# Feed-forward on one core: low parts of weights to VectorE, maximum to ScalarE, Silu as one function, smaller pieces between products

## The chip, the cores and the metric

The kernel runs on one core of one Trainium2 chip. The metric is the device time of one execution in microseconds. The kernel before was timed three times: 859.63, 856.85 and 858.03 us, a median of 858.03 us.

## What is computed

Clustered attention over 2 batches, 8 heads, 768 positions of width 64, and then two feed-forward layers on the 1536 x 512 result. The part that the change touches:

```
# first feed-forward: 512 -> 2048 -> 512
h = x @ w_in
g = np.maximum(h, 0.0) + np.log1p(np.exp(-np.abs(h)))
x = g @ w_out
# second: 512 -> 1536 -> 512
g = x @ w_gate
silu = g * (1.0 / (1.0 + np.exp(-g)))
out = (silu * (x @ w_val)) @ w_out
```

The four weights arrive in float64, the rest in float32.

## The kernel before, in words

Every float32 operand of a product is split into a high part, which TensorE takes in its rounded float32 form (`F32R`), and a low part, what is left; a product is three products (high x high, high x low, low x high), all into one PSUM bank.

A weight of 128 x 512 numbers is loaded as pairs of 32-bit words, narrowed to float32 by integer work and split. `w_narrow` takes the absolute value of the upper words on ScalarE (L122), clamps and shifts on VectorE (L123, L126) and joins the words on VectorE (L130, L133). `w_split` casts the high part `whi` on VectorE (L142) and subtracts for the low part `wlo` on GpSimd (L143). There are two buffers for the narrowed weight `m`, three for the loaded words and three or four for each split weight.

The first feed-forward works in 16 units (`h_unit`, 128 hidden columns each) and 8 groups (`y_group`, two units each). A unit is 36 matmuls of 128 x 512 (L738) into three PSUM banks; ScalarE writes |h| from each bank (L795) and VectorE max(h, 0) (L796); then exp and log on ScalarE (L799, L800), the sum on VectorE (L803), and the split of the sum: a cast on ScalarE (`gh`, L776) and a subtraction on GpSimd (`gl`, L777). A y group has four pieces of 18 matmuls (L820) into three banks each; VectorE adds every bank to an accumulator (L834); the first group is copied by ScalarE (L832), and the last group also splits the finished accumulator (`YH`, `YL`; L836, L838). PSUM's eight banks go round: a bank is used again eight allocations later. So in the middle of the stage TensorE does two units (72 matmuls) and then four pieces (72 matmuls), 144 matmuls in all; below this is called a group of the stage. Units 0 and 1 come first, units 2g+2 and 2g+3 before y group g.

The second feed-forward is built alike: 12 units (`a_unit`) of a gate and a value product, sigmoid on ScalarE (L882), two multiplies on VectorE (L883, L894), a split (L900 on ScalarE, L901 on GpSimd), and 6 groups of output products (L920) with accumulation on VectorE (L932).

The order on each engine is the order in which the program is written: every engine takes its instructions one after the other. Weight work and the softplus tails are small tasks in one queue (`todo`), which `pump` takes from after each half of a unit and after each piece: two tasks if more than four are waiting, else one. A weight is two tasks, `first` (L122, L123, L126) and `second` (L130, L133, L142, L143, and the next weight's load on the SyncE queue). A unit adds two: `log_part` (L799, L800) and `sum_part` (L803, L776, L777). With the two weights of a unit they are queued as log, first and second of an output weight, sum, first and second of an input weight. `need` takes tasks out of turn until a weight or a split sum that a product asks for is there; `first_do` puts the last two units' tails ahead of all but a weight that has begun.

Of the kernel before, what the change touches and what calls it, by code (L numbers as in the profile page):

```python
# [15 lines left out]
AF = mybir.ActivationFunctionType  # L16
ALU = mybir.AluOpType
# [12 lines left out]
def _r(t):  # L30

    return t.bitcast(F32)
# [8 lines left out]
def kernel(  # L41
# [18 lines left out]
    nc = tc.nc  # L60
# [48 lines left out]
    def w_narrow(loaded):  # L109

        raw, shape, wide = loaded
        if not wide:
            yield
            yield raw
            return
        lo, hi = raw[:, :, :, 0], raw[:, :, :, 1]  # L120
        m = wp.tile(shape, I32, tag="m", name="m", bufs=2)
        nc.scalar.activation(out=m.bitcast(F32), in_=hi.bitcast(F32), func=AF.Abs)  # L122
        nc.vector.tensor_scalar(  # L123
            out=m.bitcast(F32), in0=m.bitcast(F32), scalar1=F64_LEAST, scalar2=F64_MOST, op0=ALU.max, op1=ALU.min
        )
        nc.vector.tensor_scalar(  # L126
            out=m, in0=m, scalar1=3, scalar2=0x3FFFFFF8, op0=ALU.logical_shift_left, op1=ALU.bitwise_and
        )
        yield
        nc.vector.scalar_tensor_tensor(  # L130
            out=m, in0=hi, scalar=-0x40000000, in1=m, op0=ALU.bitwise_and, op1=ALU.bitwise_or
        )
        nc.vector.scalar_tensor_tensor(  # L133
            out=m, in0=lo, scalar=29, in1=m, op0=ALU.logical_shift_right, op1=ALU.bitwise_or
        )
        yield m.bitcast(F32)

    def w_split(x, pool, tag, bufs):
        shape = list(x.shape)
        hi = pool.tile(shape, F32R, tag="h" + tag, name="whi", bufs=bufs)  # L140
        lo = pool.tile(shape, F32R, tag="l" + tag, name="wlo", bufs=bufs)
        nc.vector.tensor_copy(hi, x)  # L142
        nc.gpsimd.tensor_tensor(out=lo, in0=x, in1=_r(hi), op=ALU.subtract)  # L143
        return hi, lo

    def cols_of(w, f):
# [9 lines left out]
    def first_of(u):  # L156
        if u < NF1:
            return [(("in", u), cols_of(w_in, u), "a")]
        if u < NU:
            return [(("gate", u - NF1), cols_of(w_gate, u - NF1), "a"), (("val", u - NF1), cols_of(w_val, u - NF1), "c")]  # L160
        return []
# [15 lines left out]
    batches = [first_of(u) for u in range(3)] + [batch_of(u) for u in range(NU)]  # L177
# [9 lines left out]
            loaded_t[stream[n_load[0]][0]] = w_load(*stream[n_load[0]][1])  # L187
            n_load[0] += 1

    begun = set()  # L190

    def split_tasks(batch):

        steps = {}

        def first(key):
            while key not in loaded_t:
                load_ahead(len(loaded_t) + 1)
            steps[key] = w_narrow(loaded_t.pop(key))
            next(steps[key])  # L200

        def second(key, tag):
            x = next(steps[key])
            load_ahead(3)
            pool, bufs = pool_of[tag]
            W[key] = w_split(x, pool, tag, bufs)

        tasks = []
        for key, _, tag in batch:
            tasks.append(functools.partial(first, key))  # L210
            tasks.append(functools.partial(second, key, tag))
            begun.add(tasks[-1])
        return tasks


    todo = collections.deque()

    def first_do(tasks):

        begun_one = [todo.popleft()] if todo and todo[0] in begun else []  # L220
        todo.extendleft(reversed(begun_one + tasks))

    def pump(n=None):
        for _ in range(n or (2 if len(todo) > 4 else 1)):
            if todo:
                todo.popleft()()

    def need(table, key):
        while key not in table:
            todo.popleft()()  # L230
        return table[key]
# [393 lines left out]
    for half in range(2):  # L625
# [5 lines left out]
        for hh in range(2):  # L631
            g = 2 * C * hh
            if half == 0:
                nc.vector.tensor_scalar(
                    out=QT[hh][64:64 + C, 0, cols], in0=_r(ps)[g:g + C, 0:384], scalar1=FAR, scalar2=-FAR,
# [3 lines left out]
            else:  # L639
                nc.scalar.copy(KT[hh][64:64 + C, 0, cols], _r(ps)[64 + g:64 + g + C, 0:384])  # L640
                nc.scalar.activation(
                    out=QT[hh][64:64 + C, 0, cols], in_=_r(ps)[g:g + C, 0:384], func=AF.Identity,
# [89 lines left out]
    def proj(xh, xl, w, banks, kks):  # L732

        hi, lo = w
        for kk in kks:
            for wt, xt, last in ((hi, xh, 0), (hi, xl, 0), (lo, xh, 1)):
                for c in range(NCH):
# [5 lines left out]
                        stop=(kk == KD - 1 and last == 1),  # L743
                    )


    h0 = [bank() for _ in range(NCH)]
    w0 = need(W, ("in", 0))
# [24 lines left out]
    def split_g(g, tag):  # L773
        gh = gp.tile([128, NTOK], F32R, tag="gh", name=tag + "h")
        gl = gp.tile([128, NTOK], F32R, tag="gl", name=tag + "l")
        nc.scalar.copy(gh, g)  # L776
        nc.gpsimd.tensor_tensor(out=gl, in0=g, in1=_r(gh), op=ALU.subtract)  # L777
        return gh, gl
# [5 lines left out]
    def h_unit(f, banks=None):  # L784
        if banks is None:
            banks = [bank() for _ in range(NCH)]
            w = need(W, ("in", f))
            for half in range(2):
                proj(XH, XL, w, banks, range(2 * half, 2 * half + 2))
                pump()  # L790
        e = tp.tile([128, NTOK], F32, tag="e", name="e")
        r = tp.tile([128, NTOK], F32, tag="s", name="r")
        for c in range(NCH):
            cs = slice(512 * c, 512 * c + 512)
            nc.scalar.activation(out=e[:, cs], in_=banks[c], func=AF.Abs)  # L795
            nc.vector.tensor_scalar_max(r[:, cs], banks[c], 0.0)  # L796

        def log_part():
            nc.scalar.activation(out=e, in_=e, func=AF.Exp, scale=-1.0)  # L799
            nc.scalar.activation(out=e, in_=e, func=AF.Ln, bias=1.0)  # L800

        def sum_part():
            nc.vector.tensor_tensor(out=e, in0=r, in1=e, op=ALU.add)  # L803
            g_t[f] = split_g(e, "g")

        return [log_part, sum_part], split_tasks(batches.pop(0))

    def y_group(g):
        last = g == NF1 // 2 - 1
# [30 lines left out]

    soft0, split0 = h_unit(0, h0)
    soft1, split1 = h_unit(1, h1)
    todo.extend(split0 + [soft0[0], soft1[0], soft0[1], soft1[1]] + split1)
    pump(6)
    for g in range(NF1 // 2):
        if 2 * g + 2 < NF1:
            for f in (2 * g + 2, 2 * g + 3):
                soft, split = h_unit(f)
                if f < NF1 - 2:
                    todo.extend([soft[0]] + split[:2] + [soft[1]] + split[2:])  # L850
                else:
                    first_do(soft + split[:2])
                    todo.extend(split[2:])
        else:
            YH = keep.tile([128, KD, NTOK], F32R, tag="xh", name="YH")
            YL = keep.tile([128, KD, NTOK], F32R, tag="xl", name="YL")
        y_group(g)
# [6 lines left out]
    def a_unit(f):  # L864
        gb = [bank() for _ in range(NCH)]
        wg = need(W, ("gate", f))
        vb = None
        if f == 0:
            vb = [bank() for _ in range(NCH)]
            wv = need(W, ("val", f))  # L870
            proj(YH, YL, wg, gb, range(KD - 1))
            proj(YH, YL, wv, vb, range(KD - 1))
            proj(YH, YL, wg, gb, range(KD - 1, KD))
            proj(YH, YL, wv, vb, range(KD - 1, KD))
        else:
            for half in range(2):
                proj(YH, YL, wg, gb, range(2 * half, 2 * half + 2))
                pump()
        sg = tp.tile([128, NTOK], F32, tag="e", name="sg")
        for c in range(NCH):  # L880
            cs = slice(512 * c, 512 * c + 512)
            nc.scalar.activation(out=sg[:, cs], in_=gb[c], func=AF.Sigmoid)  # L882
            nc.vector.tensor_tensor(out=sg[:, cs], in0=gb[c], in1=sg[:, cs], op=ALU.mult)  # L883
        if vb is None:
            vb = [bank() for _ in range(NCH)]
            wv = need(W, ("val", f))
            for half in range(2):
                proj(YH, YL, wv, vb, range(2 * half, 2 * half + 2))
                pump()
        ah = gp.tile([128, NTOK], F32R, tag="gh", name="ah")  # L890
        al = gp.tile([128, NTOK], F32R, tag="gl", name="al")
        for c in range(NCH):
            cs = slice(512 * c, 512 * c + 512)
            nc.vector.tensor_tensor(out=sg[:, cs], in0=vb[c], in1=sg[:, cs], op=ALU.mult)  # L894
            if f == NF2 - 1:
                nc.scalar.copy(ah[:, cs], sg[:, cs])
                nc.vector.tensor_tensor(out=al[:, cs], in0=sg[:, cs], in1=_r(ah)[:, cs], op=ALU.subtract)

        def split_part():
            nc.scalar.copy(ah, sg)  # L900
            nc.gpsimd.tensor_tensor(out=al, in0=sg, in1=_r(ah), op=ALU.subtract)  # L901
            a_t[f] = (ah, al)

        if f < NF2 - 1:
            todo.append(split_part)
        else:
            a_t[f] = (ah, al)
        if batches:
            todo.extend(split_tasks(batches.pop(0)))
# [67 lines left out]
```

## Time and profile before

| | |
|---|---|
| median of three runs | 858.03 us |
| profiled execution | 860.54 us |
| its span (first to last instruction) | 858.4 us |
| mean granted TensorE clock | 0.984 |
| TensorE matmul busy (PE) | 815.9 us, 95% |
| VectorE (DVE) | 686.3 us, 80% |
| ScalarE (ACT) | 397.7 us, 46% |
| GpSimd (POOL) | 336.1 us, 39% |

The span has three stages: attention to about 264 us, the first feed-forward to about 559, the second to about 855. Times in rows are microseconds from the start of the span, durations microseconds or, where marked mean, nanoseconds. A number in square brackets behind a row of the timeline is the idle time of that engine just before, with what ended it.

### The profile page before, as it was taken

What the parts mean: (1) busy time and instruction counts of PE and PEld (TensorE: products, weight loads), DVE (VectorE), ACT (ScalarE), POOL (GpSimd) and SP (SyncE); (2) the same over time, 40 slices, a digit from 0 to 9 for tenths busy, and PEclk for the clock granted to TensorE, in tenths of its full rate; (3) what the DMA queues carried; (4) which work ended last, traced back from release to release, by engine and by line L of the source; (5) the groups of instructions that cost most, each with busy time, mean ns of one, the idle gap of its engine ahead of it and who ended that gap; (6) DMA issues with size and microseconds to landing.
All of it is one profiled execution on the core that took longest, in us unless ns stands there. A gap on an engine that the chain in (4) does not pass through costs nothing.

```text
span 858.4 us, 11743 instructions
## 1 busy us (share of the span) xinstructions
PE 815.9 (95%) x4366; PEld 700.4 (82%) x4366; DVE 686.3 (80%) x1016; ACT 397.7 (46%) x735; POOL 336.1 (39%) x229
## 2 busy tenths in 40 slices
PE   7899999999999899989898997899999999999998
PEld 6899999999888678768677786678888888888886
DVE  6889988898886778898888887848886868876464
ACT  4589888988883755434244434133312213120210
POOL 4636565545421645444244333324433222332110
PEclk9899999999999999999999998999999999999999
DMA  8966776575212132122121120102222221211003
GB/s 201 263 144 148 184 169 145 131 178 119 71 38 69 52 95 74 56 76 82 59 73 50 49 74 25 49 25 74 74 74 74 74 74 50 74 56 43 1 1 147
DMA packets 65336, 75.42 MB, mean 88 GB/s; under 512 B 28960, under 2 KB 51584, under 8 KB 65280
## 3 DMA queue, kind: packets, MB, share of 16 engines
q1 hardware_dynamic: 65280, 74.68, 31.7%
q8 instruction: 34, 0.56, 0.3%
q14 instruction: 22, 0.18, 0.1%
HBM read 48.27 MB, written 3.19 MB: 60 GB/s over the span
## 4 chain that ended last, share of the span: by engine, by line
PE 66%; DVE 24%; issue 4%; ACT 3%; DMA 2%; POOL 1%; SPq 0%; DVEq 0%; POOLq 0%; ACTq 0%
PE bank L738 29%; PE bank L920 11%; PE ops L522 7%; PE tps L505 6%; PE sps L473 6%; DVE m L123 5%; DVE acc L834 4%; PE bank L820 3%; DVE e L803 3%; DVE m L133 2%; DVE r L796 2%; DVE m L130 2%; PE sims L384 2%; DVE whi L142 1%; DVE m L126 1%
## 5 line engine op out<-in xcount | busy, mean ns | idle before, releaser
L143 POOL TENSOR_TENSOR wlo<-m,whi 128x512 fp32r<-128x512 f32 x68 | 100.6, 1480 | 290.2 <-DVE whi L142 275.4
L123 DVE TENSOR_SCALAR m<-m 128x512 f32<-128x512 f32 x68 | 87.0, 1279 | 38.0 <-ACT m L122 38.0
L512 DVE TENSOR_TENSOR tl<-tps,th 128x384 fp32r<-128x384 f32 x192 | 98.9, 551 | 16.4 <-ACT th L511 16.0
L481 DVE TENSOR_REDUCE nm<-sps 128x1 f32<-128x768 f32 x96 | 91.4, 953 | 14.2 <-PE sps L473 11.3
L505 PE MATMUL tps<-id,p 128*128 128x128 f32 x576 | 94.5, 281 | 1.0 <-DVE tl L512 1.0
L511 ACT CAST th<-tps 128x384 fp32r<-128x384 f32 x192 | 84.7, 492 | 20.1 <-PE tps L505 17.3
L489 ACT ACTIVATE p<-sps,nm 128x768 f32<-128x768 f32 x96 | 88.3, 920 | 5.2 <-DVE nm L481 5.1
L473 PE MATMUL sps<-KT,QT 128*128 128x384 f32 x384 | 84.1, 341 | 5.8 <-ACT p L489 5.0
L738 PE MATMUL bank<-YH,whi 128*128 128x512 f32 x288 | 81.7, 392 | 2.6 <-DVE acc L834 2.6
L505 PEld LDWEIGHTS tps<-id,p 128*128 128x128 f32 x576 | 76.3, 153 | 7.8 <-DVE tl L512 4.3
L738 PE MATMUL bank<-YL,whi 128*128 128x512 f32 x288 | 81.4, 391 | 0.0
L738 PE MATMUL bank<-YH,wlo 128*128 128x512 f32 x288 | 81.3, 391 | 0.0
L522 PE MATMUL ops<-th,VV 128*128 128x256 f32 x288 | 80.6, 308 | 0.0
L776 ACT CAST gh<-e 128x1536 fp32r<-128x1536 f32 x16 | 23.7, 1481 | 121.8 <-DVE e L803 121.8
L820 PE MATMUL bank<-gh,whi 128*128 128x512 f32 x192 | 58.2, 404 | 17.7 <-DVE r L796 8.6
L522 PE MATMUL ops<-tl,VV 128*128 128x256 f32 x288 | 73.2, 283 | 0.0
L122 ACT ACTIVATE m<-raw 128x512 f32<-128x512 f32 x68 | 44.3, 663 | 61.2 <-POOL wlo L143 61.2
L777 POOL TENSOR_TENSOR gl<-e,gh 128x1536 fp32r<-128x1536 f32 x16 | 57.2, 3579 | 36.2 <-ACT gh L776 32.4
L473 PEld LDWEIGHTS sps<-KT,QT 128*128 128x128 f32 x384 | 63.8, 191 | 6.6 <-ACT p L489 5.6
L738 PEld LDWEIGHTS bank<-YH,whi 128*128 128x128 f32 x288 | 54.5, 189 | 14.3 <-issue 3.0
L738 PEld LDWEIGHTS bank<-YL,whi 128*128 128x128 f32 x288 | 54.5, 189 | 11.4
L738 PEld LDWEIGHTS bank<-YH,wlo 128*128 128x128 f32 x288 | 54.4, 189 | 11.3
(124 smaller groups left out, 1778.6 us busy)
## 6 DMA issues: line engine op xcount, KB each, us to landing
raw<-in_moe_w_out_dram SPq DMA_DIRECT2D x28, 512.0 KB, 3.3
raw<-in_moe_w_in_dram SPq DMA_DIRECT2D x16, 512.0 KB, 3.8
QT<-hi SPq DMA_DIRECT2D x32, 192.0 KB, 3.0
raw<-in_moe_w_val_dram SPq DMA_DIRECT2D x12, 512.0 KB, 4.7
raw<-in_moe_w_gate_dram SPq DMA_DIRECT2D x12, 512.0 KB, 3.4
KT<-hi SPq DMA_DIRECT2D x14, 384.0 KB, 4.2
qn<-in_q_dram SPq DMA_DIRECT2D x16, 192.0 KB, 4.9
kn<-in_k_dram SPq DMA_DIRECT2D x16, 192.0 KB, 3.7
```

Of the source, the lines that this page charges most:

```text
L123: nc.vector.tensor_scalar(out=m.bitcast(F32), in0=m.bitcast(F32), scalar1=F64_LEAST, scalar2=F64_MOST, op0=ALU.max, op1=ALU.min)
L143: nc.gpsimd.tensor_tensor(out=lo, in0=x, in1=_r(hi), op=ALU.subtract)
L473: nc.tensor.matmul(ps[:, c, 0:384], lhsT=Q[:, a, 128 * j:128 * j + 128], rhs=K[:, a, 384 * c:384 * c + 384], start=(a == 0), stop=(a == 1),)
L481: nc.vector.tensor_reduce(out=nm, in_=ps[:, :, 0:384], axis=AX.XY, op=ALU.max, negate=True)
L489: nc.scalar.activation(out=_h(p), in_=s_t.pop(i)[:, :, 0:384], func=AF.Exp, bias=nm_t.pop(i), accum_out=sm_t[pr][:, j:j + 1],)
L505: nc.tensor.transpose(ps[:, 128 * j:128 * j + 128], p[:, 128 * kb:128 * kb + 128], id32)
L511: nc.scalar.copy(th, pv)
L512: nc.vector.tensor_tensor(out=tl, in0=pv, in1=_r(th), op=ALU.subtract)
L522: nc.tensor.matmul(o[:, 0:CW], lhsT=VV_t[pr][:, hh, kb].rearrange("p a d -> p (a d)"), rhs=t[:, kb, :], start=(kb == 0 and lohi == 0), sto ...
L738: nc.tensor.matmul(banks[c], lhsT=wt[:, kk, :], rhs=xt[:, kk, 512 * c:512 * c + 512], start=(kk == 0 and wt is hi and xt is xh), stop=(kk ...
L820: nc.tensor.matmul(banks[NCH * d + c], lhsT=wt[:, 0, ds_], rhs=gt[:, 512 * c:512 * c + 512], start=(ff == 0 and n == 0), stop=(ff == 1 and ...
L920: nc.tensor.matmul(bk, lhsT=lhs[:, ts_], rhs=rhs[:, 0, :], start=(ff == 0 and n == 0), stop=(ff == 1 and n == 2),)
```

## The change

Five edits: (1) from the first feed-forward on, `wlo` is subtracted on VectorE; (2) from unit 3 on, max(h, 0) is a Relu on ScalarE; (3) Silu is one function of ScalarE, in place of a sigmoid and a multiply on VectorE; (4) a weight has three tasks: L122 alone, then L123 and L126, then the rest; the softplus tail has three: log, sum, split; (5) `pump` takes up to three tasks where more than twelve are waiting; a first task of a weight is not counted, and is also taken at the end of a turn when it stands next.

```diff
         nc.scalar.activation(out=m.bitcast(F32), in_=hi.bitcast(F32), func=AF.Abs)
+        yield
         nc.vector.tensor_scalar(
...
+    low_on = [nc.gpsimd]
...
-        nc.gpsimd.tensor_tensor(out=lo, in0=x, in1=_r(hi), op=ALU.subtract)
+        low_on[0].tensor_tensor(out=lo, in0=x, in1=_r(hi), op=ALU.subtract)
...
-        def second(key, tag):
+        def second(key):
+            next(steps[key])
+
+        def third(key, tag):
             x = next(steps[key])
...
             tasks.append(functools.partial(first, key))
-            tasks.append(functools.partial(second, key, tag))
+            firsts.add(tasks[-1])
+            tasks.append(functools.partial(second, key))
+            begun.add(tasks[-1])
+            tasks.append(functools.partial(third, key, tag))
             begun.add(tasks[-1])
...
     def pump(n=None):
-        for _ in range(n or (2 if len(todo) > 4 else 1)):
+        for _ in range(n or (3 if len(todo) > 12 else 2 if len(todo) > 4 else 1)):
+            if todo and todo[0] in firsts:
+                todo.popleft()()
             if todo:
+                todo.popleft()()
+            if todo and todo[0] in firsts and n is None:
                 todo.popleft()()
...
+    low_on[0] = nc.vector
+
 
     h0 = [bank() for _ in range(NCH)]
...
-            nc.vector.tensor_scalar_max(r[:, cs], banks[c], 0.0)
+            if f < 3:
+                nc.vector.tensor_scalar_max(r[:, cs], banks[c], 0.0)
+            else:
+                nc.scalar.activation(out=r[:, cs], in_=banks[c], func=AF.Relu)
...
             nc.vector.tensor_tensor(out=e, in0=r, in1=e, op=ALU.add)
+
+        def split_part():
             g_t[f] = split_g(e, "g")
 
-        return [log_part, sum_part], split_tasks(batches.pop(0))
+        return [log_part, sum_part, split_part], split_tasks(batches.pop(0))
...
-                    todo.extend([soft[0]] + split[:2] + [soft[1]] + split[2:])
+                    todo.extend([soft[0]] + split[:3] + [soft[1]] + split[3:6] + [soft[2]] + split[6:])
                 else:
-                    first_do(soft + split[:2])
-                    todo.extend(split[2:])
+                    first_do(soft + split[:3])
+                    todo.extend(split[3:])
...
-            nc.scalar.activation(out=sg[:, cs], in_=gb[c], func=AF.Sigmoid)
-            nc.vector.tensor_tensor(out=sg[:, cs], in0=gb[c], in1=sg[:, cs], op=ALU.mult)
+            nc.scalar.activation(out=sg[:, cs], in_=gb[c], func=AF.Silu)
```

`first_do` now leaves in front all steps of a weight that has begun (up to two) instead of one, and the tails of units 0 and 1 are queued as logs, sums, splits between the weights of the two units, with eight tasks taken at once there instead of six.

## Rows read from the trace of the kernel before

**Rows 1.** Windows by stage: length, each engine's busy time (instructions), granted clock, DMA.
```profile
264.35:559.40 295.05, 268.17 (x1136) 215.59 (x1136) 251.94 (x330) 125.71 (x154) 120.86 (x56) 0.98 0.21 64
559.40:854.60 295.20, 295.20 (x1294) 243.98 (x1294) 212.37 (x304) 60.06 (x87) 83.41 (x45) 0.99 0.18 57
```

**Rows 2.** Chain that ended last, a piece in the second feed-forward: start, length, what.
```profile
626.12 16.32 PE bank L920 x72
```

**Rows 3.** Waits in the first feed-forward: total us, times, longest us.
```profile
DVE m L123 <- ACT m L122: 27.1, 15, 3.6
...
PE bank L820 <- DVE r L796: 8.6, 4, 4.0
...
PE bank L820 <- DVE acc L834: 7.5, 5, 2.6
...
PE bank L738 <- DVE acc L834: 4.9, 3, 2.2
```

**Rows 4.** Timeline of TensorE, two of its stops.
```profile
301.60 0.50 PE L820 MATMUL bank<-gh,whi 128*128 128x512 f32 x1 [1.90 <-DVE r L796]
...
385.22 0.50 PE L738 MATMUL bank<-XH,whi 128*128 128x512 f32 x1 [2.25 <-DVE acc L834]
```

**Rows 5.** Windows around stops; the clock is the third number from the end.
```profile
290.00:310.00 20.00, 18.10 (x80) 14.67 (x79) 12.39 (x18) 13.32 (x20) 12.59 (x5) 1.00 0.19 53
...
370.00:390.00 20.00, 17.36 (x68) 13.85 (x69) 19.40 (x28) 5.49 (x5) 7.46 (x3) 0.91 0.20 65
...
512.00:560.00 48.00, 38.03 (x152) 29.51 (x151) 38.75 (x49) 13.93 (x18) 18.54 (x11) 0.93 0.16 51
```

**Rows 6.** Timeline around one sum, TensorE left out: start, length, instruction.
```profile
375.03 1.75 DVE L803 TENSOR_TENSOR e<-r,e 128x1536 f32<-128x1536 f32 x1
...
376.81 1.49 ACT L776 CAST gh<-e 128x1536 fp32r<-128x1536 f32 x1 [9.80 <-DVE e L803]
...
378.38 3.52 POOL L777 TENSOR_TENSOR gl<-e,gh 128x1536 fp32r<-128x1536 f32 x1 [0.43 <-ACT gh L776]
...
378.90 3.28 DVE L123 TENSOR_SCALAR m<-m 128x512 f32<-128x512 f32 x1 [0.33 <-ACT m L122]
...
382.22 0.43 DVE L126 TENSOR_SCALAR m<-m 128x512 int32<-128x512 int32 x1
...
382.68 0.69 DVE L130 SCALAR_TENSOR_TENSOR m<-raw,m 128x512 int32<-128x512 int32 x1
...
384.13 0.43 DVE L142 CAST whi<-m 128x512 fp32r<-128x512 f32 x1
...
384.48 1.88 DVE L834 TENSOR_TENSOR acc<-bank,acc 128x512 f32<-128x512 f32 x3
...
386.27 0.42 DVE L123 TENSOR_SCALAR m<-m 128x512 f32<-128x512 f32 x1
```

**Rows 7.** Groups by line in the first feed-forward: count, busy us, mean ns, idle before.
```profile
L123 DVE TENSOR_SCALAR m<-m 128x512 f32<-128x512 f32 x36 | 53.6, 1489 | 27.1 <-ACT m L122 27.1
...
L796 DVE TENSOR_SCALAR r<-bank 128x512 f32<-128x512 f32 x48 | 30.0, 681 | 6.1 <-ACT e L795 6.1
...
L126 DVE TENSOR_SCALAR m<-m 128x512 int32<-128x512 int32 x36 | 26.1, 724 | 1.2
...
L795 ACT ACTIVATE e<-bank 128x512 f32<-128x512 f32 x48 | 25.0, 594 | 13.9 <-PE bank L738 12.0 <-POOL gl L777 1.9
```

**Rows 8.** Groups by line in the second feed-forward.
```profile
L883 DVE TENSOR_TENSOR sg<-bank,sg 128x512 f32<-128x512 f32 x36 | 22.6, 681 | 22.0 <-ACT sg L882 22.0
...
L897 DVE TENSOR_TENSOR al<-sg,ah 128x512 fp32r<-128x512 f32 x3 | 2.1, 693 | 2.1 <-ACT ah L896 2.1
...
L882 ACT ACT_TABLE_LOAD x1 | 1.3, 1283 | 0.0
```

**Rows 9.** Timeline: the same subtraction on GpSimd and on VectorE at one time.
```profile
565.16 1.30 POOL L838 TENSOR_TENSOR YL<-acc,YH 128x512 fp32r<-128x512 f32 x1 [0.17 <-ACT YH L836]
...
565.72 1.28 DVE L838 TENSOR_TENSOR YL<-acc,YH 128x512 fp32r<-128x512 f32 x1 [0.69 <-ACT YH L836]
```

More of the change, by code (lines that the diff above doesn't have):

```diff
@@ L122, in w_narrow @@
         nc.scalar.activation(out=m.bitcast(F32), in_=hi.bitcast(F32), func=AF.Abs)
+        yield
         nc.vector.tensor_scalar(
@@ L188, in load_ahead @@
             n_load[0] += 1
-    begun = set()
+    firsts, begun = set(), set()
     def split_tasks(batch):
@@ L218, in first_do @@
     def first_do(tasks):
-        begun_one = [todo.popleft()] if todo and todo[0] in begun else []
-        todo.extendleft(reversed(begun_one + tasks))
+        begun_ones = []
+        while todo and todo[0] in begun:
+            begun_ones.append(todo.popleft())
+        todo.extendleft(reversed(begun_ones + tasks))
     def pump(n=None):
-        for _ in range(n or (2 if len(todo) > 4 else 1)):
+        for _ in range(n or (3 if len(todo) > 12 else 2 if len(todo) > 4 else 1)):
+            if todo and todo[0] in firsts:
+                todo.popleft()()
             if todo:
+                todo.popleft()()
+            if todo and todo[0] in firsts and n is None:
                 todo.popleft()()
@@ L842 @@
     soft1, split1 = h_unit(1, h1)
-    todo.extend(split0 + [soft0[0], soft1[0], soft0[1], soft1[1]] + split1)
-    pump(6)
+    todo.extend(split0 + [soft0[0], soft1[0], soft0[1], soft1[1], soft0[2], soft1[2]] + split1)
+    pump(8)
     for g in range(NF1 // 2):
```

## The prediction

> **What bounds the kernel now.** I read the stretches first. From 559.40 to 854.60 TensorE is busy for all of 295.20 us [rows 1], at the full-speed spacing of 16.32 us for 72 matmuls, 0.2267 us each [rows 2]: the second feed-forward hides everything else, and edits there can only cost. From 264.35 to 559.40, the first feed-forward, TensorE is busy for 268.17 of 295.05 us, so it stands idle for 26.9 us; its 1136 matmuls at full spacing are 257.5 us, so the busy time holds another 10.7 us of slow matmuls. 37.5 us is all that can be won there. Who ends the idle time: the waits say VectorE, 8.6 us for `r` (the maximum with zero), 7.5 and 4.9 us for `acc` [rows 3], that is, for PSUM banks that VectorE empties late. The slow matmuls follow long stops: after the stop of 1.90 us [rows 4] the granted clock stayed at 1.00, after 2.25 us it was 0.91 over the window, and over the 48 us with the longest stop, 4.0 us [rows 3], 0.93 [rows 5], the engine falling from 2.4 to 1.2 GHz for a while; 0.09 of 20 us is 1.8 us for such a fall.
>
> Why VectorE is late stands in the timeline [rows 6]. After the sum (375.03, 1.75 us) the next task in the queue is the beginning of another weight. Its `m` (L122) is on ScalarE behind `gh`, 1.49 us, so VectorE's L123 starts 2.1 us after the sum; by then `gl` (378.38, 3.52 us) runs on GpSimd, and L123 lasts 3.28 us, ending with it, where it takes 0.42 us alone. So one sum costs VectorE about 5 us. Over the stretch: L123 1.489 us in the mean, x36, against 0.42 alone is 38.5 us; L126, 0.724 against 0.43, 10.6 us (beside `wlo` on GpSimd) [rows 7]; waiting for `m` 27.1 us [rows 3].
>
> A check: one group (two h units and the four y pieces, 144 matmuls, 32.64 us of TensorE) asks of VectorE twelve evictions of `acc` (1.88 us for three: 7.5), two sums (3.5), six maxima (3.76), four weights of 0.42+0.43+0.69+0.69+0.43 (L133 like L130 [rows 6]) and 0.03 between them (11.2): 26.0. With an eighth of 49 us held and of 27.1 us waiting it is 35.5 us; the stretch divided by eight is 36.9. VectorE is the bound of the first feed-forward.
>
> **The change, part by part.**
> Maximum to ScalarE, units 3 to 15: takes 13 times 1.88 = 24.4 us from VectorE, 3.76 per group. ScalarE pays three ACTIVATEs from PSUM, nearest row `Abs` at 0.594 shown, about 0.53 behind each other [rows 7]: 1.6 us a unit, 20.6 in all, on an engine busy 125.7 of 295 us [rows 1]. Hidden as long as a unit's `Abs` and maximum (3.2 us) aren't stuck behind a `gh` that waits for a sum; without that cover a bank comes late by that wait. The wait for `r` goes; the bank is then freed by ScalarE, which waits for products 12.0 us in the stretch [rows 7]. The Trainium skill ("ScalarE: Activation LUTs", Rules for kernel authors) says the opposite, maximum on VectorE. By that rule the 24.4 us stay on VectorE and a group asks 3.76 us more of it than below; here rows decide, 0.594 against 0.681 from PSUM, on the engine that has time.
>
> Low parts to VectorE: 36 weights in this stretch [rows 7]. VectorE's own subtraction of this shape is 0.693 us (`al`, L897) [rows 8], 0.65 in a queue: 23.4 us, 2.6 a group. Bounds: 0.6, and 1.28 as beside a GpSimd subtraction [rows 9]; I take 0.65, because a low part follows a cast that has then already waited. It takes `wlo` off GpSimd, so L126's 10.6 us go.
>
> Pieces: the `Abs` is now issued ahead of its pump's end, and `gh`/`gl` are a task of their own after the next weight. So most of the 27.1 us go (I keep up to 2 us a group, where `Abs` sits behind log and exp, two ACTIVATEs of `gh`'s size [rows 6], 3 us). The holding does not go: ScalarE does not wait for the pump, so `gh` still starts when the sum ends, and `gl` covers 1.6 to 5.1 us after it. What now meets it is not L123 (0.1 to 0.5) but L142, the cast, at 2.4: VectorE loses about 2.9 us per sum instead of 5, between 0 (where evictions fill the time) and 3.5 (`gl`'s length). Twice a group: 5.8.
>
> VectorE per group after: 7.5 + 3.5 + four weights of 3.46 (13.8) = 24.8, held 5.8, waiting 0 to 2: 31 to 33 against TensorE's 32.64. TensorE is the bound again, barely, and bursts decide the rest.
>
> The bursts, from the order of the queue. With over 12 tasks waiting a pump takes three. After y piece 0 of groups 1, 2 and 4 these are the sum, and both other steps of an output weight. Take the end of that piece as 0: `acc` to 1.9, sum to 3.6, L123 and L126 to 4.5, L130 and L133 to 6.0, L142 held until 8.7 and done at 9.1, low part 9.8, first bank of the next `acc` 10.5. TensorE has eight banks and takes three per piece: it wants that bank at the third matmul of piece 3, at 2 x 4.08 + 0.45 = 8.6. A stop of 1.9 us. Groups 3 and 5 begin with steps of a weight and lose less, about 1.5; I take 9 us for the five.
> Start: the stop of 1.90 us at 301.60 [rows 4] waits for unit 3's `r`, which ScalarE now writes; with smaller ones before it I leave 1 us.
> End: from 512 to 560 us TensorE's 152 matmuls need 34.5 of 48 us [rows 5]: 13.5 us lost. The stop of 4.0 us waited for `r` [rows 3] and goes. In the last y group a piece asks of VectorE 1.88 for `acc`, 0.7 of waiting for `YH` (a cast like `whi`'s, on ScalarE) and 0.7 for `YL` (as L897 [rows 8]): 3.3. Four pieces are 13.2, two more weights 6.9, held some 2 beside GpSimd's part of `YL` (1.30 [rows 9]): 22 against TensorE's 16.3, 6 late, with 1 brought along 7 us.
> Slow clock: two stops over 2.25 us, 1.8 us each: 3.6.
> Left: 1 + 9 + 7 + 3.6 = 20.6 of 37.5. Gain 17.
>
> Second feed-forward: low parts add 30 x 0.65 = 19.5 us, Silu in one function removes 36 multiplies of 0.63 (22.7) [rows 8]: nothing, on an engine busy 212 of 295 us. ScalarE's Silu I price as the sigmoid; one table load of 1.28 us stands in the shadow of the first product [rows 8]; even two per unit would be 31 us on an engine busy 60 of 295 [rows 1]. Attention keeps its order (its two pumps still take one weight each).
>
> Sum: the profiled execution 860.54 (span 858.4), less 17 is 843.5; it lies 2.5 above the median of 858.03, so the forecast is 841 for the median.
>
> **The rivals.**
> (1) Bursts are absorbed: `gl` meets evictions, not the cast; stops only at start and end, 8 us and one fall of the clock, 9.8 left. Gain 27.5, 830.5. For: 31 us against 32.6; against: `gh` follows the sum by itself.
> (2) Stops of 1.9 grow just over 2.25 us, and each brings the slow clock: 2.3 + 1.8 in five groups are 20.5, 1 + 7 at the ends with 3.6 of slow clock: 32 left. Gain 5.5, 852.5. For: 1.90 and 2.25 lie close, my count of the cast is good to some 0.3 us.
> (3) Slower: three tasks per pump put the bank's release behind a burst in every middle group, each a stop as long as the longest of now, 4.0 us, and 1.8 of slow clock: six groups 34.8, start and end 8 and 3.6: 46.4 left, 9 more than now, 867. It decides once a middle group loses over (37.5 - 11.6)/6 = 4.3 us. Against: VectorE would have to ask over 36.9 us a group, and `gl` alone can hold it for no more than 7.
> (4) Nothing: ScalarE, now alone on the h banks, sits behind a waiting `gh`, so that the 20 us that TensorE waits for `r` and `acc` [rows 3] come back as waits for ScalarE: 37 left, 858.
>
> **How the numbers follow.** Forecast 0.55 (own range 833 to 848), (1) 0.18, (2) 0.15, (3) 0.07, (4) 0.05. A measurement tells 0.3%, 2.6 us. Faster 0.88, same 0.05, slower 0.07. The range leaves out the outer quarters of (1) and (2), and (3) and (4): 827 to 853.
>
> **What would show it.** Right: the second feed-forward busy throughout; L126 at 0.43 everywhere; L123's mean under 0.8; waits of TensorE for `r` gone after unit 2; casts (L142) of 2 to 3 us beside `gl`; stops under 2 us at the third matmul of a piece 3; first feed-forward 275 to 280 us. Wrong: TensorE waiting for `e` or `r` of ScalarE, a granted clock under 0.95 in many slices, the casts at 0.43 throughout, or idle TensorE after 560 us.

## The result

The changed kernel takes 845.36 us (median of four runs, 844.71 to 847.81) against 858.83 us for the kernel before on the same chip: a ratio of 0.9844 (0.9806 to 0.9883). The forecast was 841 us, the range 827 to 853. The profiled execution, the slowest of the four, took 847.81 us, its span 846.0 us. In the changed kernel's lines L756 is the projection, L845 the y piece, L123 the absolute value, L125 and L128 clamp and shift, L132 and L135 the joins, L148 the cast `whi`, L149 the low part `wlo`, L796 `gh`, L797 `gl`, L826 the sum, L859 `acc`, L817 and L819 the maximum on VectorE and on ScalarE.

Windows of the two feed-forwards, as in [rows 1]:

```profile
264.93:547.27 282.34, 266.47 (x1136) 216.44 (x1136) 245.98 (x327) 145.74 (x193) 65.94 (x20) 0.97 0.22 67
547.27:842.18 294.91, 294.90 (x1294) 243.74 (x1294) 196.87 (x298) 60.14 (x87) 42.88 (x14) 1.00 0.17 57
```

The first went from 295.05 to 282.34 us; the second still has TensorE busy throughout. Of the 24.8 us above the 257.5 us of full-speed matmuls, 15.9 are idle time. What ended most of it, to be read against [rows 3]:

```profile
PE bank L845 <- DVE acc L859: 6.6, 5, 1.8
PE bank L756 <- DVE acc L859: 4.2, 2, 3.3
PE bank L845 <- DVE r L817: 3.2, 1, 3.2
```

The other 1.9 us are two waits for the cast `whi`. One wait for `r` is left, and the stops for `acc` are six of at most 1.8 us and a last one of 3.3. The window of [rows 3] ends before the last stop of the kernel before, the one at 559.40 us; from 264 to 560 us that kernel shows

```profile
PE bank L738 <- DVE acc L834: 7.5, 4, 2.6
```

so the last stop has grown, from 2.6 to 3.3 us. VectorE's groups, against [rows 7]:

```profile
L148 DVE CAST whi<-m 128x512 fp32r<-128x512 f32 x36 | 38.7, 1074 | 1.8
L125 DVE TENSOR_SCALAR m<-m 128x512 f32<-128x512 f32 x36 | 31.0, 860 | 20.9 <-ACT m L123 20.8
L149 DVE TENSOR_TENSOR wlo<-m,whi 128x512 fp32r<-128x512 f32 x36 | 24.9, 692 | 1.9
...
L128 DVE TENSOR_SCALAR m<-m 128x512 int32<-128x512 int32 x36 | 19.5, 542 | 1.2
```

The clamp fell from a mean of 1489 to 860 ns and the shift from 724 to 542, but the cast, 0.43 us alone, now has a mean of 1074: (1.074 - 0.43) x 36 = 23.2 us. Much of the holding moved from the clamp to the cast, and little of it went: the clamp is still held for (0.860 - 0.42) x 36 = 15.8 us and the shift for 4.0, 43 us in all against 49 before. Of the 16 `gl`, seven now meet a cast (3.6 us each) and five a clamp alone (3.3 to 3.7). The chain of waits of the changed kernel around a stop shows it (start, length, what):

```profile
375.46 1.67 DVE e L826
377.13 0.35 DVE m L125
...
377.96 0.70 DVE m L132
...
378.69 0.71 DVE m L135
...
379.42 3.64 DVE whi L148
...
383.08 0.69 DVE wlo L149
383.77 0.61 DVE acc L859
...
384.43 1.65 PE bank L845 x6
```

The 6.6 us from the clamp to the end of the low part stand between a sum and the `acc` that TensorE waits for, and 3.64 of them are one cast.

### The profile page after: what moved, and what is told of

Same layout as the page of the kernel before. It is cut to its first block, busy times and chain, and to the rows that moved or that the text cites. A ratio compares the mean times of both kernels' runs of the same rounds, so it can differ in the third digit from the quotient of the medians.

```text
span 846.0 us, 11685 instructions
## 1 busy us (share of the span) xinstructions
PE 817.6 (97%) x4366; PEld 704.3 (83%) x4366; DVE 663.1 (78%) x1007; ACT 417.7 (49%) x774; POOL 240.7 (28%) x163
## 4 chain that ended last, share of the span: by engine, by line
PE 75%; DVE 16%; DMA 4%; ACT 2%; issue 2%; POOL 1%; SPq 0%; POOLq 0%; DVEq 0%; ACTq 0%
PE bank L756 34%; PE bank L944 12%; PE bank L845 8%; PE ops L540 6%; PE sps L491 6%; PE tps L523 6%; DVE acc L859 3%; DVE whi L148 2%; DVE m L125 2%; PE sims L402 2%; DMA rd<-R 2%; DVE m L135 1%; DMA R<-rd 1%; DVE e L826 1%; DVE m L132 1%
## 5 line engine op out<-in xcount | busy, mean ns | idle before, releaser
L797 POOL TENSOR_TENSOR gl<-e,gh 128x1536 fp32r<-128x1536 f32 x16 | 59.9, 3746 | 204.7 <-ACT gh L796 191.6
L925 POOL TENSOR_TENSOR al<-sg,ah 128x1536 fp32r<-128x1536 f32 x11 | 38.6, 3507 | 207.0 <-ACT ah L924 207.0
L529 ACT CAST th<-tps 128x384 fp32r<-128x384 f32 x192 | 84.7, 491 | 20.6 <-PE tps L523 18.0
L491 PE MATMUL sps<-KT,QT 128*128 128x384 f32 x384 | 86.6, 348 | 4.1 <-ACT p L507 2.3
L756 PE MATMUL bank<-YH,whi 128*128 128x512 f32 x288 | 81.4, 390 | 3.3 <-DVE acc L859 3.3
L125 DVE TENSOR_SCALAR m<-m 128x512 f32<-128x512 f32 x68 | 58.9, 866 | 31.4 <-ACT m L123 31.3
L756 PE MATMUL bank<-YL,whi 128*128 128x512 f32 x288 | 81.5, 392 | 0.0
L756 PE MATMUL bank<-YH,wlo 128*128 128x512 f32 x288 | 81.4, 391 | 0.0
L123 ACT ACTIVATE m<-raw 128x512 f32<-128x512 f32 x68 | 44.5, 667 | 72.7 <-DVE wlo L149 72.7
L918 DVE TENSOR_TENSOR sg<-bank,sg 128x512 f32<-128x512 f32 x36 | 22.8, 684 | 60.8 <-PE bank L756 60.8
L491 PEld LDWEIGHTS sps<-KT,QT 128*128 128x128 f32 x384 | 65.5, 196 | 5.4 <-ACT p L507 3.2
L845 PE MATMUL bank<-gh,whi 128*128 128x512 f32 x192 | 58.0, 407 | 11.0 <-DVE acc L859 6.6
L756 PEld LDWEIGHTS bank<-YH,whi 128*128 128x128 f32 x288 | 54.2, 188 | 15.0 <-issue 3.7
L756 PEld LDWEIGHTS bank<-YH,wlo 128*128 128x128 f32 x288 | 54.5, 189 | 11.4
L756 PEld LDWEIGHTS bank<-YL,whi 128*128 128x128 f32 x288 | 54.5, 189 | 11.3
```

The source lines that it names most:

```text
L125: nc.vector.tensor_scalar(out=m.bitcast(F32), in0=m.bitcast(F32), scalar1=F64_LEAST, scalar2=F64_MOST, op0=ALU.max, op1=ALU.min)
L491: nc.tensor.matmul(ps[:, c, 0:384], lhsT=Q[:, a, 128 * j:128 * j + 128], rhs=K[:, a, 384 * c:384 * c + 384], start=(a == 0), stop=(a == 1),)
L529: nc.scalar.copy(th, pv)
L756: nc.tensor.matmul(banks[c], lhsT=wt[:, kk, :], rhs=xt[:, kk, 512 * c:512 * c + 512], start=(kk == 0 and wt is hi and xt is xh), stop=(kk ...
L845: nc.tensor.matmul(banks[NCH * d + c], lhsT=wt[:, 0, ds_], rhs=gt[:, 512 * c:512 * c + 512], start=(ff == 0 and n == 0), stop=(ff == 1 and ...
```

## The experiments

Each ratio is to runs of the kernel before on the same chip, with its 95% interval. Rows come from different chips, whose medians of the kernel before lie between 858.48 and 859.96 us, so a difference of two rows in microseconds is good to some 1.5 us.

| kernel | us | ratio |
|---|---|---|
| changed | 845.36 | 0.9844 (0.9806 to 0.9883) |
| maximum on VectorE | 854.84 | 0.9957 (0.9942 to 0.9971) |
| low parts on GpSimd | 832.35 | 0.9697 (0.9678 to 0.9717) |
| pieces as before | 855.36 | 0.9969 (0.9955 to 0.9984) |
| sigmoid and multiply | 843.96 | 0.9840 (0.9796 to 0.9884) |
| pieces alone | 838.51 | 0.9747 (0.9706 to 0.9787) |
| gate for `gl`, one tile more | 849.74 | 0.9891 (0.9867 to 0.9914) |
| gate for `gl`, no tile more | 835.34 | 0.9717 (0.9679 to 0.9756) |
| low parts on GpSimd, split at once | 839.00 | 0.9769 (0.9752 to 0.9787) |
| low parts on GpSimd, unit 2 on ScalarE | 832.50 | 0.9698 (0.9679 to 0.9718) |
| `gl` on VectorE | 827.95 | 0.9640 (0.9621 to 0.9658) |
| `gl` on VectorE, low parts on GpSimd | 826.35 | 0.9599 (0.9563 to 0.9635) |
| `gl` on VectorE, empty last group | 821.90 | 0.9562 (0.9528 to 0.9597) |

**Each part undone.** First the maximum:

```diff
-            if f < 3:
+            if f < NF1:
                 nc.vector.tensor_scalar_max(r[:, cs], banks[c], 0.0)
```

> The changed kernel with the maximum with zero left on VectorE in all units. The theory that VectorE's demand decides: 3.76 us more per group of 32.6 us, about 35 instead of 31 us, so VectorE becomes the bound again and the middle groups lose 3 to 4 us each instead of 1.3: 853 to 857 us, with TensorE waiting for r again. Rival, that the order of the pieces alone frees the banks in time: 845 to 848 us, no wait for r in the middle groups.

854.84 us: as the theory of VectorE's demand had it, 9.5 us slower. TensorE's waits in this kernel:

```profile
PE bank L845 <- DVE r L817: 8.7, 3, 3.7
PE bank L845 <- DVE acc L859: 8.1, 5, 3.1
```

The waits for `r` are back at the 8.6 us of [rows 3]. A maximum on VectorE is what the Trainium skill advises ("ScalarE: Activation LUTs", Rules for kernel authors), with a figure for bf16 as its reason. For float32 out of PSUM, where VectorE is the bound and ScalarE has time, this run decides the other way, by 9.5 us. Then the low parts:

```diff
-    low_on[0] = nc.vector
+    low_on[0] = nc.gpsimd
```

> The changed kernel with the low parts of the weights left on GpSimd. Theory of VectorE's demand: 2.6 us less work per group, and about 1.3 us more held beside the low parts on GpSimd (the shift at 1.40 instead of 0.43 us in some of them): 843 to 846 us, so this edit by itself gains nothing. Rival, that GpSimd's low parts are what held VectorE: the holding comes back, 850 to 854 us.

832.35 us: both missed, and not by size alone, since neither had undoing this edit as a gain. Undoing it makes the kernel 13 us faster than the changed one. In this kernel's first feed-forward the cast is not held at all, while clamp and shift still are, by 17.7 and 11.8 us:

```profile
L125 DVE TENSOR_SCALAR m<-m 128x512 f32<-128x512 f32 x36 | 32.8, 912 | 29.3 <-ACT m L123 29.3
L128 DVE TENSOR_SCALAR m<-m 128x512 int32<-128x512 int32 x36 | 27.3, 758 | 1.2
L148 DVE CAST whi<-m 128x512 fp32r<-128x512 f32 x36 | 16.3, 453 | 1.8
```

and no TensorE stop is left between 305 and 513 us. The same place in the queue, first with low parts on GpSimd (VectorE, ScalarE's `gh` and GpSimd only; start, length, instruction):

```profile
340.28 1.49 ACT L796 CAST gh<-e 128x1536 fp32r<-128x1536 f32 x1 [4.02 <-DVE e L826]
...
342.53 0.43 DVE L148 CAST whi<-m 128x512 fp32r<-128x512 f32 x1
...
343.04 1.30 POOL L149 TENSOR_TENSOR wlo<-m,whi 128x512 fp32r<-128x512 f32 x1 [6.36 <-DVE whi L148]
...
344.30 3.52 POOL L797 TENSOR_TENSOR gl<-e,gh 128x1536 fp32r<-128x1536 f32 x1
```

and then in the changed kernel:

```profile
340.78 1.49 ACT L796 CAST gh<-e 128x1536 fp32r<-128x1536 f32 x1 [4.01 <-DVE e L826]
...
342.34 4.03 POOL L797 TENSOR_TENSOR gl<-e,gh 128x1536 fp32r<-128x1536 f32 x1 [9.31 <-ACT gh L796]
343.03 3.63 DVE L148 CAST whi<-m 128x512 fp32r<-128x512 f32 x1
...
346.70 0.69 DVE L149 TENSOR_TENSOR wlo<-m,whi 128x512 fp32r<-128x512 f32 x1
...
348.04 0.50 PE L845 MATMUL bank<-gh,whi 128*128 128x512 f32 x1 [1.82 <-DVE acc L859]
```

In the first, GpSimd's queue has the weight's low part in front of `gl`, since the new order of tasks puts the split behind the next weight; the low part waits for the cast, and `gl` with it. In the second nothing stands in front of `gl`: it starts as soon as `gh` is there, 0.69 us before the cast, and the cast ends only after it. The cast takes 3.63 us there against 0.43. The Trainium skill describes such a lock ("SBUF — State Buffer", Who interferes with whom): of a VectorE instruction in a mode that takes both port pairs and a GpSimd instruction, whoever starts first has the shared pair for its whole length, and the other waits. The trace agrees, with 3.63 us. So the low part on GpSimd is a gate: it keeps `gl` from starting before the cast is done. Next the pieces:

```diff
 # the kernel before, with
+    low_on[0] = nc.vector
...
+                nc.scalar.activation(out=r[:, cs], in_=banks[c], func=AF.Relu)
...
+            nc.scalar.activation(out=sg[:, cs], in_=gb[c], func=AF.Silu)
```

> The kernel before with three of the edits (low parts on VectorE, maximum on ScalarE, Silu as one function) but its tasks and pump as they were. Theory: the clamp behind a sum again waits 2.1 us for its absolute value behind the cast gh and is held to the end of gl, 5 us a sum instead of 3: VectorE asks some 35 us per group, 852 to 856 us. Rival, that the pieces only reorder the same work: 845 to 848 us.

855.36 us, as the theory had it. The clamp is held as in [rows 7], 1433 against 1489 ns, and waits 31.6 us for `m`, where the changed kernel waits 20.8 (L123 in this kernel's lines):

```profile
L123 DVE TENSOR_SCALAR m<-m 128x512 f32<-128x512 f32 x36 | 51.6, 1433 | 31.6 <-ACT m L122 31.6
```

And Silu:

```diff
-            nc.scalar.activation(out=sg[:, cs], in_=gb[c], func=AF.Silu)
+            nc.scalar.activation(out=sg[:, cs], in_=gb[c], func=AF.Sigmoid)
+            nc.vector.tensor_tensor(out=sg[:, cs], in0=gb[c], in1=sg[:, cs], op=ALU.mult)
```

> The changed kernel with the sigmoid and the multiply on VectorE instead of Silu. Theory: TensorE is busy throughout the second feed-forward with 22.7 us of VectorE work more, since VectorE is then busy some 235 of 295 us: 845 us within 1.5. Rival, that the low parts on VectorE need the room: stops in the second feed-forward, 849 us or more.

843.96 us, not to be told from the changed kernel. TensorE is busy for 295.31 of the second feed-forward's 295.33 us with the multiplies too: an edit in a stage where TensorE is always busy is worth nothing.

**The pieces alone.** New tasks and pump; the maximum and the sigmoid's multiply on VectorE, low parts on GpSimd.

```diff
 # the changed kernel, with
+    low_on[0] = nc.gpsimd
+            if f < NF1:   # maximum on VectorE in all units
+            nc.scalar.activation(out=sg[:, cs], in_=gb[c], func=AF.Sigmoid)
...
```

> The kernel before with the pieces alone: new tasks and pump, but low parts on GpSimd, maximum on VectorE, sigmoid and multiply. Theory of VectorE's demand: 26.0 us per group, held and waiting some 6 instead of 9.5: 843 to 849 us. Rival, that without the moves of work the order changes nothing: 855 to 859 us.

838.51 us, better than the theory and 7 us better than the whole change. Of the five edits the pieces gain some 20 us, the maximum (with Silu, which gains nothing above) 4 to 6 more (832.35), and the low parts lose 13. Which of the pieces' own parts gains the 20 us (the absolute value as a task by itself, the later split, up to three tasks at once) was not tried one by one; only the later split is taken up below.

**Is it the gate?** A copy of one column makes `gl` wait for the newest low part, with the low parts on VectorE:

```diff
             W[key] = w_split(x, pool, tag, bufs)
+            last_lo[0] = W[key][1]
...
+    gate_t = keep.tile([128, 1], F32, name="gate_t")
...
         nc.scalar.copy(gh, g)
+        nc.gpsimd.tensor_copy(gate_t, _r(last_lo[0])[:, 0, 0:1])
         nc.gpsimd.tensor_tensor(out=gl, in0=g, in1=_r(gh), op=ALU.subtract)
```

> The changed kernel, low parts on VectorE, with a copy of one column of the newest low part on GpSimd in front of each gl, so that gl cannot start before that weight's cast is done. Theory, that the low parts on GpSimd were a gate: in the changed kernel gl starts as soon as gh is there and holds the cast (3.6 us, 7 times); with the gate the cast is at 0.43 us, the three stops of 1.8 us and their slow clock go, 833 to 838 us. Rival, that the 2.6 us of low parts per group on VectorE make the stops: they stay, 844 to 846 us.

849.74 us, a miss. The mechanism was there, though, in this kernel's timeline:

```profile
340.39 0.43 DVE L148 CAST whi<-m 128x512 fp32r<-128x512 f32 x1
...
341.68 0.18 POOL L800 COPY gate_t<-wlo 128x1 f32<-128x1 f32 x1 [11.66 <-DVE wlo L149]
...
341.82 3.52 POOL L801 TENSOR_TENSOR gl<-e,gh 128x1536 fp32r<-128x1536 f32 x1
```

The stops in the middle were gone too. What was new stood in the second feed-forward, where nothing had been edited. In the same 100 us, this kernel:

```profile
600.00:700.00 100.00, 100.00 (x430) 80.58 (x429) 68.86 (x108) 19.31 (x28) 14.10 (x4) 1.00 0.19 64
```

430 matmuls, where the changed kernel makes 443, at the same granted clock of 1.00; 72 matmuls of an output product take 16.80 us instead of 16.32. I had added a tile of 4 bytes per partition, which moves the tiles behind it. So the copy was given the kernel's unused padding tile to write to:

```diff
-    keep.tile([128, 96], F32, name="fill")
+    fill = keep.tile([128, 96], F32, name="fill")
...
-    gate_t = keep.tile([128, 1], F32, name="gate_t")
+    gate_t = fill[:, 0:1]
```

> As the kernel with the gate (a copy of one column of the newest low part on GpSimd in front of each gl), but the copy goes into the unused padding tile that the kernel already has, so that no tile after it moves in SBUF. In the gate run the casts were no longer held and the stops of 1.8 us were gone, yet each matmul came 0.233 instead of 0.227 us after the one before, with the granted clock at 1.00, in all stages behind the attention. Theory, that the extra tile's four bytes moved the operands: matmuls at 0.227 us again and 833 to 839 us. Rival, that the gate itself slows TensorE: 847 to 851 us.

835.34 us, as the theory had it, and in the same window

```profile
600.00:700.00 100.00, 100.00 (x443) 82.81 (x442) 70.03 (x111) 19.65 (x28) 14.04 (x4) 1.00 0.22 69
```

The 72 matmuls take 16.32 us again. The gate alone brings 10 of the 13 us back, with the low parts still on VectorE: most of the loss is what their leaving set free, not their 0.69 us of work. The counter-test leaves the low parts on GpSimd and puts `gl` in front of the next one:

```diff
-todo.extend([soft[0]] + split[:3] + [soft[1]] + split[3:6] + [soft[2]] + split[6:])
+todo.extend([soft[0]] + split[:3] + [soft[1], soft[2]] + split[3:6] + split[6:])
```

> The changed kernel with the low parts on GpSimd (832.35 us) and the split of the softplus sum queued right behind the sum instead of behind the next weight, so that gl stands in front of that weight's low part in GpSimd's queue. Theory of the gate: gl starts with gh again, the cast behind the sum is held, stops come back: 840 to 847 us. Rival, that only the place of the low parts matters: 831 to 834 us.

839.00 us: 6.7 us lost, just under the theory's range. The stops are back, but with `gl` early it is the clamp that is held (a mean of 1625 ns), not the cast as the theory had it:

```profile
L125 DVE TENSOR_SCALAR m<-m 128x512 f32<-128x512 f32 x36 | 58.5, 1625 | 25.5 <-ACT m L123 25.5
```

This kernel, which has no gate, is still 6.4 us faster than the changed one. So the work of the low parts on VectorE has a share too; the 10 us of the gate and these 6.4 overlap, and no run parts them cleanly.

**The start.** In the changed kernel the wait for `r` is here (timeline, VectorE, GpSimd and the stop):

```profile
290.08 7.12 POOL L797 TENSOR_TENSOR gl<-e,gh 128x1536 fp32r<-128x1536 f32 x2 [30.82 <-ACT gh L796]
...
292.27 1.60 DVE L125 TENSOR_SCALAR m<-m 128x512 f32<-128x512 f32 x1 [2.11 <-ACT m L123]
...
293.91 3.58 DVE L128 TENSOR_SCALAR m<-m 128x512 int32<-128x512 int32 x1
...
297.41 1.87 DVE L817 TENSOR_SCALAR r<-bank 128x512 f32<-128x512 f32 x3
...
298.14 0.79 PE L845 MATMUL bank<-gh,whi 128*128 128x512 f32 x1 [3.15 <-DVE r L817]
```

Two `gl` one behind the other hold a clamp and a shift, and the maximum of unit 2, which stays on VectorE, comes after both. So, on the 832.35 us kernel:

```diff
-            if f < 3:
+            if f < 2:
                 nc.vector.tensor_scalar_max(r[:, cs], banks[c], 0.0)
```

> The changed kernel with the low parts on GpSimd and the maximum of unit 2 on ScalarE as well. At the start VectorE's maximum of unit 2 stands behind a clamp and a shift that two gl hold (1.5 and 3.6 us), and TensorE stops 1.9 us for it. Theory: that stop goes, while the stop of 1.8 us that follows, for ScalarE's maximum of unit 3, grows by no more than 1.5: 830 to 832 us. Rival, that ScalarE at the start is the bound: 832 to 834 us, the two stops together as long as before.

832.50 us (830.66 to 834.72): nothing. In its trace the two stops at the start, 1.94 and 1.83 us, have become one of 2.35 us that waits for ScalarE: the stop for unit 2's maximum went, as the theory had it. But the granted clock from 290 to 310 us is 0.91, where it was 1.00 with the two stops, and 0.09 of 20 us is 1.8 us, more than the 1.4 us that the stops gave. Whether the clock takes it back in every execution, one trace of each kernel does not show.

**No holding by `gl`.** `gl` on VectorE:

```diff
-        nc.gpsimd.tensor_tensor(out=gl, in0=g, in1=_r(gh), op=ALU.subtract)
+        nc.vector.tensor_tensor(out=gl, in0=g, in1=_r(gh), op=ALU.subtract)
```

> The changed kernel with gl, the low part of the softplus sum, on VectorE too, so that GpSimd computes nothing in the first feed-forward. Theory of holding: VectorE does 3.5 us more per group but is held by nothing there, 28 against 31 us; clamp, shift and cast at 0.43 us throughout, no stop in the middle groups, a smaller one at the start: 830 to 837 us. Rival, that VectorE's amount of work decides: 846 to 852 us.

827.95 us, better than the theory's 830 to 837: 16 subtractions of 1.75 us more on the engine that was the bound, and the kernel is 17 us faster, since what they did to it from GpSimd is gone:

```profile
L797 DVE TENSOR_TENSOR gl<-e,gh 128x1536 fp32r<-128x1536 f32 x16 | 28.0, 1752 | 5.1 <-ACT gh L796 5.1
L128 DVE TENSOR_SCALAR m<-m 128x512 int32<-128x512 int32 x36 | 16.4, 454 | 1.2
L148 DVE CAST whi<-m 128x512 fp32r<-128x512 f32 x36 | 16.3, 453 | 1.8
L125 DVE TENSOR_SCALAR m<-m 128x512 f32<-128x512 f32 x36 | 15.2, 421 | 9.6 <-ACT m L123 9.6
```

The same with the low parts on GpSimd (both edits above together):

```diff
-    low_on[0] = nc.vector
+    low_on[0] = nc.gpsimd
...
+        nc.vector.tensor_tensor(out=gl, in0=g, in1=_r(gh), op=ALU.subtract)
```

> Low parts of the weights on GpSimd, gl on VectorE, the rest as changed. Theory of VectorE's demand: 2.6 us less work per group than with both on VectorE (827.95 us) and about 1.3 us held beside the low parts; TensorE is the bound either way, so 826 to 829 us. Rival, that any GpSimd work beside VectorE's clamp, shift and cast brings stops back: 831 to 836 us.

826.35 us, as expected: the intervals of the two overlap. Once `gl` is off GpSimd, where the low parts are hardly matters.

**The end.** On the 827.95 us kernel:

```diff
-            pump()
+            if not last:
+                pump()
```

> gl on VectorE as in the 827.95 us kernel, and no task taken from the queue in the last y group, so that its two weight steps run in the second feed-forward. Theory, that the last stop (3.3 us, and 1.7 us of slow clock) is VectorE's load in the last group, 22 us against 16.3: without the weight it is 13 us, 823 to 826 us. Rival, that the stop is the way from the last products over acc, YH and YL, which no weight is on: 827 to 829 us.

821.90 us, the lowest median of all. Its only waits of TensorE in the first feed-forward:

```profile
PE bank L845 <- ACT r L819: 1.1, 1, 1.1
PE bank L756 <- DVE whi L148: 0.7, 1, 0.7
```

The last stop of 3.3 us is gone, and so is its slow clock (0.96 from 500 to 540 us in the 827.95 us kernel, 1.00 here). It was the load of two weight steps on VectorE, not the way over `acc`, `YH` and `YL`: the theory was right, and its 823 to 826 us a little too high. Low parts on GpSimd with this end was not tried.

## Why the prediction was right, and where it was not

**The bound.** Right. TensorE stays busy through the second feed-forward, and every gain above is in the first.

**The burst.** Right in place and, for groups 1, 2 and 4, in size. Their stop was forecast at 1.9 us at the third matmul of piece 3, with the cast held by `gl`; it came there, as 1.82, 1.82 and 1.81 us, with the cast at 3.6 us instead of my 3.1. The other two middle groups lost 0.9 and nothing: 6.3 us for the five instead of 9.

**The start.** Too small: forecast 1 us, measured stops of 0.7 and 3.15 us. The stop of [rows 4] did wait for unit 3's `r`, and it is gone: it stood at the 21st matmul of the first y group, on a bank that unit 3 had used. What I missed is a new stop at that group's third matmul, on a bank of unit 2, whose `r` stays on VectorE behind two instructions that two `gl` hold.

**The end.** 5.7 us of stops for a forecast of 7.

**Slow clock.** Forecast 3.6 us; in this execution the busy time holds 9.0 us more than full-speed matmuls. After the start's stop the granted clock was 0.83 over 20 us (1.00 is 2.4 GHz throughout, less means stretches at 1.2), and two of the three stops of 1.8 us also brought 0.91, the third did not:

```profile
290.00:310.00 20.00, 16.85 (x61) 13.29 (x61) 17.17 (x22) 15.04 (x23) 8.34 (x3) 0.83 0.17 53
335.00:355.00 20.00, 18.18 (x73) 14.52 (x72) 18.88 (x26) 7.35 (x9) 4.03 (x1) 0.91 0.19 57
375.00:395.00 20.00, 18.18 (x81) 14.73 (x80) 19.62 (x26) 6.30 (x6) 4.04 (x1) 1.00 0.17 52
440.00:460.00 20.00, 18.19 (x74) 14.59 (x72) 18.84 (x27) 7.39 (x9) 4.02 (x1) 0.91 0.20 60
```

The 9.0 us belong to this execution, though: the mean granted clock of the four is 0.980 in this one and 0.986 to 0.992 in the others. The kernel with sigmoid and multiply has the same first feed-forward, and its trace the same stops to 0.02 us, 15.9 us in all; yet its stage is 277.8 us long, its slow matmuls are 4.4 us, and the clock fell after none of the three:

```profile
262.30:540.07 277.77, 261.91 (x1136) 213.16 (x1135) 245.83 (x327) 145.65 (x193) 65.98 (x20) 0.99 0.22 69
331.00:351.00 20.00, 18.19 (x81) 14.72 (x80) 18.86 (x26) 7.35 (x9) 4.03 (x1) 1.00 0.19 58
369.40:389.40 20.00, 18.19 (x81) 14.74 (x80) 19.62 (x26) 6.33 (x6) 4.02 (x1) 1.00 0.17 52
434.40:454.40 20.00, 18.18 (x81) 14.73 (x80) 18.83 (x27) 7.36 (x9) 4.03 (x1) 1.00 0.22 59
```

So the line that I drew between 1.90 and 2.25 us is none: the same stop brought a fall in one execution and not in another, and in the 832.35 us kernel a last stop of 2.60 us was followed by 1.00. Rival (2), which asked a stop of over 2.25 us, had a part of the truth in this execution and none in the other. What decides stays open.

**The sum.** Altogether 24.8 us are left above full speed in this execution for a forecast of 20.6, and 20.3 in that of the sigmoid kernel; the gain was 13.5 us in the medians for a forecast of 17. The stops alone are 15.9 us for a forecast of 17, but by errors that cancel: 2.7 us too much for the bursts and 1.3 for the end, 2.9 too little for the start. That they cancel is luck. Three signs of being right did not come: L126 (now L128) at 0.43 everywhere (its mean is 0.542), the clamp's mean under 0.8 (0.860), and casts of 2 to 3 us (3.6). The first feed-forward at 275 to 280 us did not come in this execution (282.3) and did in that of the sigmoid kernel (277.8).

**The low parts, right for half a reason.** I priced them at 2.6 us per group for VectorE against the shift's holding that goes with `wlo`. Both came about: 0.69 us each, and the shift held only beside `gl` and `YL`. I also saw that `gl` would now meet the cast. What I did not see is that this very edit lets it: I wrote that `gl` follows the sum by itself, and took GpSimd's queue, with a low part that waits for the cast, for no more than load. The edit that I counted as nearly even costs 13 us.

**The maximum and the pieces.** Right that both are needed: without either, 854.8 and 855.4 us. What the pieces do is less sure. Of the 27.1 us of waiting for `m` I kept at most 16; 20.8 are left, and the 832.35 us kernel, 13 us faster, has 29.3. The total of that waiting does not tell the time; where it falls would have to be followed stop by stop.

## What to carry to other kernels

Before work is moved off an engine, ask what waits behind it there: an instruction that waits for the right thing may be all that keeps a long one from starting at the wrong time. Where two engines lock each other out, count the time that the one holds the other and not the work alone: 28 us of subtraction moved onto the bound engine made it 17 us faster. Undo a change part by part even when it gains, for one part of five lost nearly as much as the whole had won. And read a stage's slow clock from more than one execution: here the same stops went with 9.0 us of it and with 4.4.

## What the runs showed of the hardware

- One more tile of 4 bytes per partition, in a pool ahead of others, cost 14.4 us (849.74 against 835.34 us) with the same instructions: the matmuls came 0.233 instead of 0.227 us apart at a granted clock of 1.00 (16.80 against 16.32 us for 72). The two were timed on different chips; the kernel with `gl` on VectorE, timed on the chip of the slower one, kept 16.32. Which operand's place does it was not tried.
- Stops of TensorE of 1.81 and 1.82 us were followed by a granted clock of 0.91 in two places and of 1.00 in a third; in an execution of another kernel with the same first feed-forward, the same three stops were followed by 1.00 each time.
- A cast of 0.43 us on VectorE took 3.63 us where a GpSimd subtraction of 128x1536 numbers had started 0.69 us before it; seven casts of the changed kernel took 3.61 to 3.63 us so.
